# A transformer block on one core: tile 3's LayerNorm taken behind the start of K, scale sums ahead of tile 2's transposes, a matmul pair split 3 to 5

## Chip, cores, metric

One core of one Trainium2 chip. The time is the device time of a whole execution in microseconds.

Engines: PE (TensorE) multiplies, DVE (VectorE) and ACT (ScalarE) work on elements, POOL (GpSimd) does a few small operations, SP issues the loads.

## The reference, cut to what matters

A diffusion-transformer block on 2 batches of 256 tokens, width D = 1152, two heads, hidden width 4 D:

```python
mod = (_silu(c) @ w_mod).reshape(B, 6, 1, D)
shift_a, scale_a, gate_a, shift_m, scale_m, gate_m = [mod[:, i] for i in range(6)]
h = _layernorm(x) * (1 + scale_a) + shift_a
qkv = (h @ wqkv).reshape(B, N, 3, H, Dh)
# ... attention, output projection, second LayerNorm, two-layer MLP
```

Only the first 20 us matter here: LayerNorm of four 128-token tiles (0 and 1 are batch 0, 2 and 3 batch 1), their transposes, the scale sums `silu(c) @ w_mod` for `scale_a`, and the first matmuls of K, the key projection. A k-tile is one of the nine slices of 128 features over which these matmuls sum.

## The kernel before: the parts concerned

The builder keeps one list of instructions per engine and puts semaphore waits between them. PE runs exactly in the order in which the program names its units; the early orders of DVE and ACT are fixed by lists. Waits are per PSUM bank (PSUM is where PE's results land). `hk` multiplies one k-tile by its scale, and K's matmuls read its result. The program of PE before (cuts marked `...`):

```python
def sca(k0, k1):            # scale sums of weight rows k0..k1: 4 tiny matmuls per row
    for kt in range(k0, k1): mod_f0(kt)                  # feature tile 0, bank 1
    for kt in range(k0, k1): mod_kt(WSC, kt, 0, ..., (1, KC))  # tiles 1 to 3, bank 7
...
xn_T(1); sca(0, 3); warm(1, "d"); sca(3, 6); warm(1, "f", "aggr_ln1_2")
xn_T(0)                     # nine 128x128 transposes of normalised tile 0 into PSUM
warm(1, "e", "rstd_ln1_2")  # a filler matmul that keeps the clock up
xn_T(2, 0, 8)
sca(6, 9)
hk(0, 0); sc1a(0, 1, 1); sc1a(1, KC); hk(1, 0)   # DVE: scale batch 0; copy the sums
xn_T_copy(0, 4, 8, "act"); xn_T_copy(0, 8, 9, "act")       # ACT: read banks 5 and 3
hk(2, 0, "act"); hk(3, 0, "act")
xn_T(3, 0, 8)
k_first(0)                  # K, k-tile 0, batch 0: 8 matmuls into banks 0, 1, 5, 3
xn_T(3, 8, 9); xn_T(2, 8, 9)
k_first(1)
...
k_pair(range(KC), 0, 1); k_pair(range(KC), 1, 1); ...; k17(0, 0, KC)
for kt in range(KT):        # sums of the other scale features ("scb"): 9 x 5 tiny matmuls
    if kt == 6: k12(0)      # 4 matmuls of K, batch 1
    mod_kt(WSC, kt, 0, "scb_%d" % kt, (KC, KT))
hk(KC, 0)                   # DVE: scale k-tile 4, needs all the sums
...
k12(1)                      # the other 4
... k_pair((KC,), ...)      # K on k-tile 4
```

SP issues the loads in this order: x (two loads), the first half of the scale weights (`sc0`, three), K's weights for k-tiles 0 to 3, the second half of the scale weights (`sc4`, three), K's others, and so on.

Of the kernel before, what the change touches and what calls it, by code (L numbers as in the profile page):

```python
# [509 lines left out]
KC = 4  # L510
# [3 lines left out]
def c_mm(n):  # L514
    return max(n / 2.4 + 2.5, 27.0)
# [26 lines left out]
def build_kernel(nc, x, c, wqkv, wo, w_mod, w_fc1, w_fc2, out):  # L542
    S = Sched()
# [4 lines left out]
    with (  # L548
# [10 lines left out]
        def ps32(bank, c0=0, n=512):  # L559
            return psum[:, bank * 512 + c0: bank * 512 + c0 + n]  # L560
# [126 lines left out]
        def mm(o, l, r, st, sp, **kw):  # L687
            S.instr(lambda e: e.matmul(o, lhsT=l, rhs=r, start=st, stop=sp, **kw), reads=[l, r], writes=[o])  # L688

        def tr(o, i_, idn):  # L690
            S.instr(lambda e: e.transpose(o, i_, idn), reads=[i_, idn], writes=[o])  # L691
# [75 lines left out]
        def xslot(b, kt, n=256):  # L767
            return ps16(XB[b][kt // 4], (kt % 4) * 256 + (512 if kt == 8 and b == 1 else 0), n)


        def xn_T(t, ka=0, kb=KT):
            b = t // 2
            S.unit("pe", (kb - ka) * c_mm(128), "xnT_%d_%d" % (t, ka))
            for kt in range(ka, kb):
                tr(xslot(b, kt)[:, (t % 2) * 128:(t % 2) * 128 + 128], XN[:, t, kt * 128:(kt + 1) * 128], IDENT)

        def xn_T_copy(b, k0, k1, eng):
            src = xslot(b, k0, (k1 - k0) * 256).rearrange("p (k t) -> p k t", k=k1 - k0)
            copy_on(eng, HX[:, k0:k1, b * 256:(b + 1) * 256], src, (k1 - k0) * 256, True, "xnT_cp%d_%d" % (b, k0))

        def warm(n, tag, behind=None):
            for i in range(n):
                S.unit("pe", 300.0, "warm_%s_%d" % (tag, i))
                mm(ps32(0), IDENT, Q4B, True, True)
                if behind:
                    S.instrs[-1].deps.update(j for j in S.instrs[:-1] if j.name == behind)

        def mod_kt(W, kt, col0, name, fs=(0, 9)):
            S.unit("pe", (fs[1] - fs[0]) * 27.0, name)
            for f in range(*fs):  # L790
                mm(ps32(7, col0 + f * 2, 2), W[:, kt, f * 128:(f + 1) * 128], ST[:, kt:18:9], False, kt == KT - 1, skip_group_check=True)
# [6 lines left out]
        def hk(kt, b, eng="dve"):  # L798
            dst = HK[:, kt, b * 256:(b + 1) * 256]
            s1 = ps32(1 if kt == 0 else 7, 2 * kt, 1) if kt in (0, KC) and b == 0 else SC1A[:, kt * 2 + b:kt * 2 + b + 1]  # L800
            src = xslot(b, kt) if kt < KC else HX[:, kt, b * 256:(b + 1) * 256]
            if eng == "act":
                act(c_act(256, 1), lambda e: e.activation(out=dst, in_=src, func=ACTF.Copy, scale=s1), [src, s1], [dst], "hk_%d_%d" % (kt, b))
                return
            dve(345 if kt < KC else 285, lambda e: e.tensor_scalar(out=dst, in0=src, scalar1=s1, scalar2=None, op0=ALU.mult),  # L805
                [src, s1], [dst], "hk_%d_%d" % (kt, b))

        def k_mm(kts, j, b, bank, half):

            for kt in kts:  # L810
                mm(ps32(bank, half * 256, 256), WK[:, kt, j * 128:(j + 1) * 128], HK[:, kt, b * 256:(b + 1) * 256], kt == 0 and half == 0,
                   kt == KT - 1, skip_group_check=True)

        KB = [(0, 1, 5, 3), (4, 2, 6)]
        ev_rr = [0]

        def k_pair(kts, i, b, bank=None):
            S.unit("pe", 2 * len(kts) * c_mm(256), "k%d_%d_%d" % (b, i, kts[0]))
            bank = KB[b][i] if bank is None else bank
            if kts[0] == 0:  # L820
                for kt in kts:
                    for half in range(2):
                        k_mm((kt,), 2 * i + half, b, bank, half)
            else:
                for half in range(2):
                    k_mm(kts, 2 * i + half, b, bank, half)
            if kts[-1] == KT - 1:
                eng = "act" if ev_rr[0] % 2 == 0 or (i, b) == (3, 1) else "dve"
                ev_rr[0] += 1
                copy_on(eng, QK[:, 9 + 2 * i:11 + 2 * i, b * 256:(b + 1) * 256], ps32(bank).rearrange("p (j t) -> p j t", j=2), 512, False,  # L830
                        "k_ev%d_%d" % (b, i))

        def mod_f0(kt):
            S.unit("pe", 27.0, "sca0_%d" % kt)
            mm(ps32(1, 0, 2), WSC[:, kt, 0:P], ST[:, kt:18:9], False, kt == KT - 1, skip_group_check=True)

        def sca(k0, k1):
            for kt in range(k0, k1):
                mod_f0(kt)
            for kt in range(k0, k1):  # L840
                mod_kt(WSC, kt, 0, "sca_%d" % kt, (1, KC))
# [14 lines left out]
        sca(3, 6)  # L856
        warm(1, "f", "aggr_ln1_2")
        xn_T(0)
        warm(1, "e", "rstd_ln1_2")
        xn_T(2, 0, 8)  # L860
        sca(6, 9)
        hk(0, 0)
        sc1a(0, 1, 1)
        sc1a(1, KC)
# [2 lines left out]
        xn_T_copy(0, 8, 9, "act")  # L867
        hk(2, 0, "act")
        hk(3, 0, "act")
        xn_T(3, 0, 8)  # L870

        def k_first(kt):
            for i in range(4):
                k_pair((kt,), i, 0)

        k_first(0)
        xn_T(3, 8, 9)
        xn_T(2, 8, 9)
        k_first(1)
        xn_T_copy(1, 4, 8, "act")  # L880
        xn_T_copy(1, 8, 9, "act")
        for kt in range(2, KC):
# [6 lines left out]
        def k17(b, ka, kb):  # L889
            S.unit("pe", (kb - ka) * c_mm(256), "k17_%d_%d" % (b, ka))  # L890
            for kt in range(ka, kb):
                mm(ps32(7, 256 * (1 - b), 256), WK[:, kt, D - P:D], HK[:, kt, b * 256:(b + 1) * 256], b == 1 and kt == 0, kt == KT - 1,
                   skip_group_check=True)

        sc_ones(KC, KT)
        k17(0, 0, KC)
        def k12(half):
            S.unit("pe", KC * c_mm(256), "k1_2%d" % half)
            k_mm(range(KC), 4 + half, 1, KB[1][2], half)

        for kt in range(KT):
            if kt == 6:
                k12(0)
            mod_kt(WSC, kt, 0, "scb_%d" % kt, (KC, KT))
        hk(KC, 0)
        sc1a(KC, KT)
        for kt in range(KC, KT):
            for b in range(2):
                if kt > KC or b:
                    hk(kt, b)  # L910
        k12(1)
        for kt in range(KT):
            dma(WQ[:, kt, :], wqkv_v[:, kt, 0:D], P * D * 2, "ld_wq%d" % kt, run=2304)
# [44 lines left out]
        for kt in range(KT):  # L958
            for b in range(2):
# [5 lines left out]
                else:  # L965
# [4 lines left out]

        S.first = {
            "dve": ["zq4b", "c_half", "c_silu", "bn_ln1_1_0", "bn_ln1_1_1", "bn_ln1_1_2", "aggr_ln1_1", "veps_ln1_1", "bn_ln1_2_0",
                    "bn_ln1_2_1", "xn_1", "bn_ln1_2_2", "aggr_ln1_2", "veps_ln1_2", "xn_0", "var_ln1_3", "xn_2", "xn_3", "hk_0_0", "sc1a_0", "sc1a_1", "hk_1_0",
                    "hk_0_1", "hk_1_1", "hk_2_1", "hk_3_1", "hk_%d_0" % KC, "sc1a_4", "hk_%d_1" % KC] + ["hk_%d_%d" % (kt, b) for kt in range(KC + 1, KT) for b in range(2)],
            "act": ["ld_c", "c_tanh", "sum_ln1_0", "sq_ln1_0", "sum_ln1_3", "sq_ln1_3", "xnT_cp0_4", "xnT_cp0_8", "hk_2_0", "hk_3_0",
                    "xnT_cp1_4", "xnT_cp1_8"],
# [344 lines left out]
def bass_standalone__dit_block__diffusion_kernel(  # L1321
    nc: bass.Bass,
    x: bass.AP,
    c: bass.AP,
    wqkv: bass.AP,
    wo: bass.AP,
    w_mod: bass.AP,
    w_fc1: bass.AP,
    w_fc2: bass.AP,
    out: bass.AP,  # L1330
):
    build_kernel(nc, x, c, wqkv, wo, w_mod, w_fc1, w_fc2, out)
# [28 lines left out]
```

## Time and profile before

| | before |
|---|---|
| first three runs | 244.45 us median (244.39 to 244.59) |
| span of the profile | 242.9 us |
| k_first(0) starts | 12.116 us |
| first matmul on k-tile 4 | 20.226 us |
| from there to the end of the last DVE operation | 221.16 us |

Times inside a profile count from the start of the span. The two matmul starts are read from the trace's single records. A "hole" below is the time that PE stands still beyond the usual step from one matmul to the next; a load's "landing" is the moment at which its semaphore tells that its data are there. The prediction below shows the profile lines that led to it. Starts of transposes, weight loads and waits there are on the same clock.

### The profile page before, as it was taken

Reading aid. Unit: us, or ns where it says so; the run is one execution under the profiler, and the core shown is the slowest. Engines: PE = TensorE matmul, PEld = TensorE weight load, DVE = VectorE, ACT = ScalarE, POOL = GpSimd, SP = SyncE. Lnnn points to the kernel's source line nnn. Section 1 sums busy time; section 2 is a strip of 40 time slices with the busy share of each in tenths; the row PEclk is TensorE's granted clock in tenths of the full one; section 3 lists DMA queues with packets and bytes.
Section 4 is the critical chain, followed back from the end, with each engine's and each line's share of the span. In section 5 each row is a group of like instructions: output and inputs, shape, how many; then the busy total and the mean of one; then the engine's idle time right before and its main releaser. Section 6 shows DMA issues by size and latency. Waiting matters only on the chain.

```text
span 242.9 us, 4068 instructions
## 1 busy us (share of the span) xinstructions
PE 238.3 (98%) x1754; PEld 147.9 (61%) x1764; DVE 120.4 (50%) x218; ACT 67.0 (28%) x136; POOL 21.7 (9%) x39
## 2 busy tenths in 40 slices
PE   7999999999999999999999999999999999999996
PEld 2698854557667666898444444444556656566576
DVE  3824379596997899779999600000022222211112
ACT  4830350345424206983223332222000000000000
POOL 1600000000021186400000000020000000000000
DMA  6999999999995999989943498002000000000001
GB/s 236 338 381 392 391 391 391 398 413 404 390 353 165 345 388 392 391 262 398 338 148 84 170 302 330 0 15 86 0 16 19 16 16 19 16 16 16 19 21 30
DMA packets 30140, 51.59 MB, mean 212 GB/s; under 512 B 1703, under 2 KB 15787, under 8 KB 30123
## 3 DMA queue, kind: packets, MB, share of 16 engines
q1 hardware_dynamic: 29680, 50.14, 57.8%
q0 software_dynamic: 416, 1.19, 1.6%
q8 instruction: 14, 0.23, 0.4%
q14 instruction: 3, 0.02, 0.0%
q10 hardware_dynamic: 27, 0.00, 0.0%
HBM read 50.14 MB, written 1.19 MB: 211 GB/s over the span
## 4 chain that ended last, share of the span: by engine, by line
PE 94%; ACT 2%; DMA 2%; DVE 1%; issue 0%; POOL 0%; DVEq 0%
PE psum L688 93%; DMA arena<-in_x_dram 2%; PE psum L691 1%; ACT arena L749 1%; ACT arena L747 1%; POOL arena L751 0%; DVE arena L760 0%; DVE arena L805 0%; DVE arena L1284 0%; DVE arena L1285 0%; DVE arena L750 0%; DVEq L473 0%
## 5 line engine op out<-in xcount | busy, mean ns | idle before, releaser
L688 PE MATMUL psum<-arena 128*128 128x384 bf16 (+12 forms) x1665 | 234.8, 306 | 2.0 <-POOL arena L711 1.5
L688 PEld LDWEIGHTS psum<-arena 128*128 128x128 bf16 (+3 forms) x1675 | 142.7, 97 | 89.7 <-issue 4.5
L1079 DVE SCALAR_TENSOR_TENSOR arena<-arena 128x1152 f32<-128x1152 bf16 x32 | 44.7, 1414 | 0.6
L1284 DVE TENSOR_TENSOR arena<-psum,arena 128x384 f32<-128x384 f32 (+3 forms) x14 | 7.0, 501 | 68.0 <-PE psum L688 68.0
L1193 ACT ACTIVATE arena<-psum 128x512 bf16<-128x512 f32 (+1 forms) x44 | 22.4, 520 | 42.7 <-PE psum L688 42.7
L683 ACT ACTIVATE arena<-psum 128x512 bf16<-128x512 f32 (+6 forms) x37 | 19.6, 550 | 39.1 <-PE psum L688 38.2
L685 DVE CAST arena<-psum 128x512 bf16<-128x512 f32 (+3 forms) x13 | 8.2, 641 | 11.4 <-PE psum L688 11.3
L669 POOL DMA_DIRECT2D dit_scratch<-arena x3 | 1.8, 616 | 115.7 <-DVE arena L685 58.9
L1161 POOL TENSOR_TENSOR arena<-arena 128x384 f32<-128x384 f32 x12 | 10.9, 912 | 11.5 <-DVE arena L1160 9.8
L1106 DVE CAST arena<-psum 72x32 bf16<-72x32 f32 x1 | 0.2, 187 | 21.3 <-PE psum L688 21.3
L739 DVE BATCH_NORM_STATS2 arena<-arena 128x6 f32<-128x384 f32 (+1 forms) x18 | 9.4, 548 | 0.3
L1166 ACT ACTIVATE arena<-arena 128x1152 bf16<-128x1152 f32 x4 | 5.3, 1344 | 11.1 <-DVE arena L1165 11.1
L691 PEld LDWEIGHTS psum<-arena 128*128 128x128 bf16 (+1 forms) x89 | 5.8, 98 | 2.9 <-DVE arena L760 1.1
L691 PE MATMUL psum<-arena 128*128 128x128 bf16 (+1 forms) x89 | 7.3, 219 | 0.3
L1160 DVE TENSOR_TENSOR arena<-psum,arena 128x384 f32<-128x384 f32 x12 | 6.5, 552 | 1.5 <-PE psum L688 1.0
L1285 DVE TENSOR_TENSOR arena<-arena 128x384 bf16<-128x384 f32 (+3 forms) x14 | 7.0, 501 | 0.5
L1183 ACT ACTIVATE arena<-psum,arena 128x128 bf16<-128x128 bf16 x16 | 6.0, 456 | 1.7 <-PE psum L691 1.1
L1180 DVE TENSOR_SCALAR arena<-psum,arena 128x128 bf16<-128x128 bf16 x20 | 5.4, 337 | 1.9 <-PE psum L691 1.9
L1086 DVE TENSOR_REDUCE arena<-arena 128x36 f32<-128x1152 f32 x4 | 5.4, 1347 | 0.0
L1083 DVE STREAM_TRANSPOSE arena<-arena 128x1152 f32<-128x1152 f32 x4 | 5.4, 1364 | 0.0
L1009 ACT ACTIVATE arena<-psum,arena 128x256 bf16<-128x256 f32 x8 | 3.7, 472 | 1.3 <-PE psum L688 0.9
L743 POOL TENSOR_TENSOR arena<-arena 128x1 f32<-128x1 f32 x6 | 3.6, 596 | 1.6 <-DVE arena L742 1.6
(48 smaller groups left out, 45.0 us busy)
## 6 DMA issues: line engine op xcount, KB each, us to landing
arena<-in_w_fc_dram SPq DMA_DIRECT2D x9, 1152.0 KB, 7.2
arena<-in_w_fc_dram SPq DMA_DIRECT2D x4, 2592.0 KB, 17.4
arena<-in_wqkv_dram SPq DMA_DIRECT2D x18, 288.0 KB, 10.3
arena<-in_w_mod_dram SPq DMA_DIRECT2D x3, 1728.0 KB, 20.3
arena<-in_w_mod_dram SPq DMA_DIRECT2D x3, 864.0 KB, 13.9
arena<-in_w_mod_dram SPq DMA_DIRECT2D x9, 288.0 KB, 10.6
arena<-in_wqkv_dram SPq DMA_DIRECT2D x1, 2592.0 KB, 16.7
arena<-in_wo_dram SPq DMA_DIRECT2D x1, 2592.0 KB, 24.4
```

Source lines behind the costliest of these rows:

```text
L683: act(c_act(n), lambda e: e.activation(out=dst, in_=src, func=ACTF.Copy), [src], [dst], name)
L685: dve(c_dve_psum16(n) if psum16 else c_dve_psum32(n), lambda e: e.tensor_copy(dst, src), [src], [dst], name)
L688: S.instr(lambda e: e.matmul(o, lhsT=l, rhs=r, start=st, stop=sp, **kw), reads=[l, r], writes=[o])
L691: S.instr(lambda e: e.transpose(o, i_, idn), reads=[i_, idn], writes=[o])
L739: dve(550, lambda e, s=s, o=o: e.bn_stats(out=o, in_=s), [s], [o], "bn_%s_%d" % (tag, ci))
L1079: dve(1270, lambda e, w=w, s=s, acc=acc: e.scalar_tensor_tensor(out=acc, in0=w, scalar=s, in1=acc, op0=ALU.mult, op1=ALU.add), [w, s, acc] ...
L1160: dve(550, lambda e, o=o, ga=ga, x1c=x1c: e.tensor_tensor(out=x1c, in0=o, in1=ga, op=ALU.mult), [o, ga], [x1c], "wo_t1_%d_%d" % (t, ci))
L1161: S.op("pool", 930, lambda e, xs=xs, x1c=x1c: e.tensor_tensor(out=x1c, in0=x1c, in1=xs, op=ALU.add), reads=[x1c, xs], writes=[x1c], name=" ...
L1183: act(440, lambda e, o=o, dst=dst, s1=s1, s2=s2: e.activation(out=dst, in_=o, func=ACTF.Identity, scale=s1, bias=s2), [o, s1, s2], [dst], ...
L1193: act(c_act(ntok), lambda e: e.activation(out=dst, in_=o, func=ACTF.Gelu_apprx_tanh), [o], [dst], "gelu_%d_%d" % (f, tok0))
L1284: dve(c_dve_psum32(w), lambda e, o=o, gm=gm, t1=t1: e.tensor_tensor(out=t1, in0=o, in1=gm, op=ALU.mult), [o, gm], [t1], "fc2_t1_%d_%d" % ( ...
L1285: dve(c_dve_32(w), lambda e, t1=t1, x1c=x1c, ost=ost: e.tensor_tensor(out=ost, in0=t1, in1=x1c, op=ALU.add), [t1, x1c], [ost], "fc2_out_%d ...
```

## The change

Its intent is to let K start before tile 3 is normalised. The sums of rows 6 to 8 go ahead of tile 2's transposes, and the filler goes. Tile 3's normalise stands behind the scaling of batch 0 on DVE, and its transposes behind `k_first(1)`. One of four matmuls moves from before the last scale sums to behind them, where PE waits for DVE.

```diff
         xn_T(0)
-        warm(1, "e", "rstd_ln1_2")
+        sca(6, 9)
         xn_T(2, 0, 8)
-        sca(6, 9)
         hk(0, 0)
 ...
-        xn_T(3, 0, 8)
 ...
         k_first(0)
-        xn_T(3, 8, 9)
+        k_first(1)
         xn_T(2, 8, 9)
-        k_first(1)
+        xn_T(3)
 ...
-        def k12(half):
-            S.unit("pe", KC * c_mm(256), "k1_2%d" % half)
-            k_mm(range(KC), 4 + half, 1, KB[1][2], half)
+        def k12(part):
+            kts = ((range(3), ()), (range(3, KC), range(KC)))[part]
+            S.unit("pe", sum(map(len, kts)) * c_mm(256), "k1_2_part%d" % part)
+            for half in range(2):
+                k_mm(kts[half], 4 + half, 1, KB[1][2], half)
 ...
     DVE list:  - "xn_2", "xn_3", "hk_0_0", "sc1a_0", "sc1a_1", "hk_1_0",
                + "xn_2", "hk_0_0", "sc1a_0", "sc1a_1", "hk_1_0", "xn_3",
```

## The prediction

> **What bounds the kernel now.** I read the page first, then the chain of waits in order of time, then the timeline of each engine from 8 to 21 us, then the landings of the first loads.
>
> The chain that ended last is TensorE (PE) for 94% of the 242.9 us span. In order of time it looks like this around the part that the diff touches:
>
> ```profile
> 10.11 0.88 POOL arena L751
> ...
> 11.02 0.59 DVE arena L760
> 11.61 0.05 issue
> 11.66 0.62 PE psum L691 x8
> 12.28 0.87 PE psum L688 x8
> 13.15 0.11 PE psum L691 x2
> 13.26 6.62 PE psum L688 x95
> 19.89 0.29 DVE arena L805
> 20.18 0.05 issue
> 20.23 13.26 PE psum L688 x144
> ```
>
> Up to 11.61 us the end is set by tile 3's LayerNorm: POOL's rstd, DVE's normalise (L760), then its eight transposes (L691). From 11.66 us PE runs without a hole until 19.89, where one DVE scaling (hk of k-tile 4, L805) shows. After 20.23 the chain has no DMA in it, and nothing but a few 0.05 us pieces comes between the matmuls until the last output. So whatever the change saves before 20.23 should arrive at the end nearly whole, and the question is how much that is.
>
> PE's timeline before the dense part:
>
> ```profile
> 9.79 0.66 PE L691 MATMUL psum<-arena 128*128 128x128 bf16 x9
> 10.29 0.38 PE L688 MATMUL psum<-arena 128*128 128x512 bf16 x1
> 10.64 0.62 PE L691 MATMUL psum<-arena 128*128 128x128 bf16 x8
> 11.10 0.46 PE L688 MATMUL psum<-arena 128*128 128x2 bf16 x12
> 11.66 0.62 PE L691 MATMUL psum<-arena 128*128 128x128 bf16 x8
> ```
>
> That is: tile 0's transposes, one filler matmul ("warm e"), tile 2's eight transposes, the twelve scale sums sca(6,9), tile 3's eight transposes; then k_first(0) from 12.12. The weight loads show the idle time that the pipelined matmuls hide: the filler is followed by a wait, the scale sums by another, and there is a third at 20.22:
>
> ```profile
> 10.63 0.45 PEld L691 LDWEIGHTS psum<-arena 128*128 128x128 bf16 x8 [0.31 <-DVE arena L760]
> 11.65 0.45 PEld L691 LDWEIGHTS psum<-arena 128*128 128x128 bf16 x8 [0.20 <-DVE arena L760]
> 20.22 0.11 PEld L688 LDWEIGHTS psum<-arena 128*128 128x128 bf16 x2 [0.34 <-DVE arena L805]
> ```
>
> Start-to-start steps from the trace's single records: 56 ns a transpose, 109 ns a 128x256 matmul, 27 ns a 128x2 one, 216 ns the filler. Lost time by them: 10.285 + 0.216 to 10.639 is 0.138 us; the last sum at 11.389 + 0.027 to 11.659 is 0.243; 19.887 + 0.109 to 20.226 is 0.230.
>
> **What the Trainium skill says.** (1) "TensorE: Matmul & The Clock Gate", "Wait — 56ns, not 53.3ns?": N / 2.4 GHz + about 2.5 ns once warm, with a floor near 25 ns. The trace agrees (56, 109, 216 and 27 ns), so moving these instructions changes no cost; only holes count. (2) Same page, "What's actually happening": a clock at half rate until activity releases it, back after an idle window of about 3.4 us. The trace's 128x512 step falls from 427 to 216 ns at 6.4 us and never rises; dropping one filler leaves a hole of under 0.1 us, so I expect no slow clock. (3) Same page, "The cost: per-tile semaphore tail": increments serialise, 26.3 ns each. The trace's semaphore events agree in kind, 34 ns apart: the last scb matmul starts at 19.536, its increment comes at 19.853, and DVE's hk of k-tile 4 starts at 19.877. I use these offsets below. (4) "PSUM — Partial Sum Buffer", "PSUM bank collisions raise a hardware error": two engines must not be on one bank, so users guard by bank. The kernel does: K's four pairs write banks 0, 1, 5 and 3, and 5 and 3 hold the transposes that ACT is still copying. No wait of this kind shows before, but the new order meets one.
>
> **The change, part by part.** No arithmetic is added; one filler is removed.
>
> *Scale sums ahead of tile 2.* Tile 0's transposes end their turn at 10.285. The twelve sums then run 12 x 27 ns, to 10.605, where the filler and a wait stood. Their weights landed at 10.07, so this is free. Tile 2's transposes still wait for its normalise (semaphore at 10.592) and start at 10.64 as before, until 11.096. Saved here: the sums' own 0.32 us after tile 2.
>
> *Tile 3 leaves the path.* DVE finishes issuing tile 2's normalise at about 10.50. Next is now hk(0,0): the third sum increments at 10.285 + 0.211 + 2 x 0.034 = 10.564, hk runs 10.59 to 10.94 (0.349 as now). So k_first(0) can start when PE is free, at 11.096 instead of 12.116; its weights landed at 10.81. The copies sc1a follow at 10.86 and 10.92, hk(1,0) at 11.11 to 11.46, tile 3's normalise at 11.39 to 11.97.
>
> *The new wait.* ACT's two copies out of the transposes are unchanged:
>
> ```profile
> 10.48 1.30 ACT L683 ACTIVATE arena<-psum 128x1024 bf16<-128x1024 bf16 x2 [0.71 <-PE psum L691]
> ```
>
> The first ends at 11.508 (bank 5), the second at 11.783 (bank 3). PE comes to the pair in bank 5 at 11.096 + 4 x 0.109 = 11.532 and has to wait to about 11.56; to bank 3 at about 11.79 and waits to 11.835. With the slower first step after a wait, about 0.09 us is lost, and k_first(0) ends near 12.063 instead of 11.97.
>
> *Order after it.* k_first(1) needs hk(1,0) (11.46) and weights (11.57): no wait, ends 12.063 + 8 x 0.109 = 12.935. Ten transposes (tile 2's last, tile 3's nine; normalised by 11.97) take 0.56, so k_first(2) starts at 13.495 against 13.974: 0.479 us earlier. hk(2,0) and hk(3,0) on ACT are done by 12.7. Tile 3's copies and the hk of batch 1 end by about 15, ahead of their use from 15.2. So all up to the scb sums is rigidly 0.479 earlier: scb starts at 17.450.
>
> *K pair split 3 to 5.* Only three instead of four of its 109 ns matmuls stand ahead of the last fifteen scb sums, which therefore move from 19.163 to 18.578 (0.479 + 0.109 = 0.585 earlier with rounding). hk of k-tile 4 follows by the measured 0.714, at 19.29, and the first matmul on it by 0.349, at 19.64. Five matmuls after the sums fill PE to about 19.52, so the 0.230 hole becomes about 0.12.
>
> Sum: tile 3's waiting and the filler, 0.138 + 0.216 + 0.243 = 0.597; minus 0.09 to 0.12 for ACT's banks and small shifts; plus 0.109 from the smaller hole: 0.585 us. 244.45 - 0.585 = 243.87 us, a ratio of 0.9976.
>
> **The rivals.** *A DMA takes over.* The last fifteen sums read the load issued here:
>
> ```profile
> 7.42 0.94 SPq L669 DMA_DIRECT2D arena<-in_w_mod_dram  x1
> ...
> arena<-in_w_mod_dram SPq DMA_DIRECT2D x1, 480.0 KB, 11.1
> ```
>
> It lands at 18.51, 0.65 before its use now, and only 0.07 before the use I predict: a cap. PE gets the news some 0.04 later, so it could gain 0.61 at most, and each 0.1 us that the load is late is lost. That landing is already late: its two like-sized predecessors land 1.36 us apart, this one 2.73 after, with one 16 KB instruction packet of 1.15 us at 15.59 between. The fetch should move with PE and delay the same load. If the load came 0.3 later, 244.15. *ACT's banks cost more.* If bank 3 is freed 0.2 later, the loss comes straight off: 244.05. For it: ACT starts on tile 0's transposes and takes 1.30 us; against it: nothing in the diff delays it. *The shift is swallowed later.* The stream runs at about 390 GB/s whatever PE does. The last shift weights land at 29.00 against a use at 30.15, the first WQ slice at 29.76 against 33.53, its last at 41.83 against 43.9, WV at 49.36 against 53.2, the mod rows at 62.23 against 66.2. The smallest margin is 1.15 us, about twice the shift, so I expect nothing. If it happened: 244.4. *The static order changes elsewhere.* DVE's and ACT's later order comes from a model of time in the builder, which may swap a few instructions; the path is PE with holes of at most 0.05, so a swap would mostly be hidden. Up to 0.5 us either way. *Scale sums late.* If the increments queue more than assumed, hk(0,0) delays k_first(0); there is 0.10 us of room (10.99 against 11.096).
>
> **Range and chances.** Best case is the cap plus noise: 243.6. Bad but plausible is that half is lost and the noise of the runs before (244.39 to 244.59) goes against it: 244.3. The whole stretch is under 1% of the time, so a move of over 2% would need a mistake of another kind, such as a load or clock upset.
>
> **What would show it.** In the changed profile: tile 2's transposes still at 10.64; hk(0,0) near 10.59; k_first(0) near 11.10 directly behind them; two small PE waits on ACT near 11.55 and 11.83; ten transposes near 12.94; the last scb sums near 18.58; hk of k-tile 4 near 19.29 and PE going on near 19.64, with a hole near 0.12 rather than 0.23; a later identical shape, 0.58 us earlier. Wrong would be: a wait on a DMA near 18.5, a wait on ACT of over 0.2, hk(0,0) after 10.75, or new holes after 20 us.

## The result

| | before | changed | ratio |
|---|---|---|---|
| first result: runs | 244.38 us (243.73 to 244.59), 6 | 244.05 us (243.61 to 244.60), 6 | 0.9989 [0.9971, 1.0008] |
| again | 244.47 us, 11 | 244.24 us, 5 | 0.9993 [0.9981, 1.0005] |
| a third time | 244.24 us, 11 | 244.11 us, 5 | 0.9996 [0.9984, 1.0008] |
| span of the first profile | 242.9 us | 242.3 us | |

A ratio is the mean time of one kernel's fast runs over that of the other's in the same rounds, so not quite the ratio of the medians beside it; the brackets are its 95% interval. Of these times and the six of a rerun of before, the mean of the 16 of the changed kernel is 244.15 us and that of the 34 of before is 244.34: a gain of 0.19 us, give or take 0.19 by the two scatters (0.33 and about 0.25 us). (Nine more runs of before, from rounds without the changed kernel, have a mean of 244.56 and are left out.) So the kernel is about 0.2 us faster if it is faster at all: each of the three intervals includes 1, and all are within 2%. The median lies in the predicted range; the forecast of 0.585 us was about three times what the times show.

The first profile seems to say otherwise. The chain of waits of the changed kernel, in order of time (start, length, what):

```profile
10.32 0.47 PE psum L688 x12
10.80 0.47 PE psum L691 x8
11.26 1.83 PE psum L688 x16
13.09 0.56 PE psum L691 x10
13.65 45.25 PE psum L688 x382
```

LayerNorm of tile 3 is gone from it: the sums, tile 2's transposes, sixteen K matmuls, ten transposes, K, and no DVE scaling at 19.9 any more. DVE's timeline shows the new order, scaling first (L805), tile 3's normalise (L760) last:

```profile
10.61 0.35 DVE L805 TENSOR_SCALAR arena<-psum 128x256 bf16<-128x256 bf16 x1 [0.25 <-PE psum L688]
10.88 0.22 DVE L795 COPY arena<-psum 128x2 f32<-128x2 f32 x2
11.14 0.35 DVE L805 TENSOR_SCALAR arena<-psum,arena 128x256 bf16<-128x256 bf16 x1
11.41 0.57 DVE L760 TENSOR_SCALAR arena<-arena 128x1152 bf16<-128x1152 bf16 x1
```

The weight loads of PE show where it still waits (in brackets the idle time before and who ended it):

```profile
10.32 0.38 PEld L688 LDWEIGHTS psum<-arena 128*128 128x128 bf16 x12 [0.17 <-DMA arena<-in_w_mod_dram]
...
11.15 0.46 PEld L688 LDWEIGHTS psum<-arena 128*128 128x128 bf16 x5
...
19.62 0.22 PEld L688 LDWEIGHTS psum<-arena 128*128 128x128 bf16 x3 [0.24 <-DVE arena L805]
```

The sums at 10.32 now wait for a DMA, which they did not in the first profile of before, and the bracket before k-tile 4 is down from 0.34 to 0.24. From the single records: k_first(0) at 11.184 (predicted 11.10), ten transposes from 12.927 (12.94), last fifteen sums at 18.564 (18.58), k-tile 4 at 19.630 (19.64), the hole before it 0.123 (0.12). From 19.630 to the last element operation it is 221.162 us, against 221.164 before. Nearly every predicted time is met, and the profiled gain is 0.6 us. Yet two inputs had moved between the two profiles: x landed at 4.77 us before and 4.33 after, and K's first weights at 10.81 and 11.05. The latter by two views, the SP timeline and the DMA issues of that moment (KB, us to landing), first of before:

```profile
3.71 0.49 SPq L669 DMA_DIRECT2D arena<-in_wqkv_dram  x1
...
arena<-in_wqkv_dram SPq DMA_DIRECT2D x1, 288.0 KB, 7.1
```

then of the changed kernel:

```profile
3.37 0.53 SPq L669 DMA_DIRECT2D arena<-in_wqkv_dram  x1
...
arena<-in_wqkv_dram SPq DMA_DIRECT2D x1, 288.0 KB, 7.7
```

3.71 + 7.1 = 10.8 and 3.37 + 7.7 = 11.1: issued earlier, landed later. A difference of two single profiles therefore contains what the loads did in those two executions, and the experiments had to separate this from the change.

### The profile page after: what moved, and what is told of

Its sections match the earlier page's. It is cut to its first block, busy times and chain, and to the rows that moved or that the text cites. A ratio compares the mean times of both kernels' runs of the same rounds, so it can differ in the third digit from the quotient of the medians.

```text
span 242.3 us, 4076 instructions
## 1 busy us (share of the span) xinstructions
PE 238.4 (98%) x1763; PEld 147.5 (61%) x1763; DVE 120.3 (50%) x218; ACT 67.0 (28%) x136; POOL 21.2 (9%) x39
## 4 chain that ended last, share of the span: by engine, by line
PE 97%; DVE 2%; POOL 0%; issue 0%; ACT 0%; DVEq 0%; POOLq 0%
PE psum L688 95%; PE psum L691 2%; DVE arena L739 1%; DVE arena L760 0%; POOL arena L711 0%; DVE arena L740 0%; DVE arena L1284 0%; DVE arena L1285 0%; POOL arena L710 0%; ACT arena L726 0%; DVE arena L727 0%; DVE arena L732 0%; DVE arena L742 0%; POOL arena L717 0%; POOL arena L715 0%
## 5 line engine op out<-in xcount | busy, mean ns | idle before, releaser
L688 PE MATMUL psum<-arena 128*128 128x384 bf16 (+10 forms) x1674 | 234.9, 306 | 1.6 <-POOL arena L711 1.5
L1161 POOL TENSOR_TENSOR arena<-arena 128x384 f32<-128x384 f32 x12 | 10.9, 910 | 10.8 <-DVE arena L1160 9.5
```

What stands on the lines that cost most here:

```text
L688: S.instr(lambda e: e.matmul(o, lhsT=l, rhs=r, start=st, stop=sp, **kw), reads=[l, r], writes=[o])
L1161: S.op("pool", 930, lambda e, xs=xs, x1c=x1c: e.tensor_tensor(out=x1c, in0=x1c, in1=xs, op=ALU.add), reads=[x1c, xs], writes=[x1c], name=" ...
```

## The experiments

My theory: before, K's start is set by tile 3's normalise, hence by x; after the change it is set by the landing of K's first weights, so the gain is the distance of two things that scatter from run to run. Rivals: each part brings its own share whatever lands when; or the gain is lost later.

All twelve gave correct results. Times from the single records of each trace, in us; "weights" is the landing of K's weights for k-tile 0, "norm 3" the end of tile 3's normalise:

| kernel | x | weights | norm 3 | k_first(0) | k-tile 4 | to the last DVE operation |
|---|---|---|---|---|---|---|
| before, first profile | 4.77 | 10.81 | 11.60 | 12.116 | 20.226 | 221.164 |
| before_again | 4.25 | 11.18 | 11.01 | 11.636 | 19.742 | 221.162 |
| only_sums | 5.08 | 11.83 | 11.90 | 12.415 | 20.522 | 221.167 |
| only_split | 4.87 | 11.35 | 11.70 | 12.210 | 20.213 | 221.162 |
| only_tile3 | 4.79 | 11.43 | 13.01 | 12.054 | 20.622 | 221.164 |
| before_late_ln3 | 4.75 | 11.25 | 12.08 | 12.596 | 20.707 | 221.163 |
| before_wkswap | 4.77 | 12.63 | 11.60 | 12.763 | 20.868 | 221.164 |
| changed, first profile | 4.33 | 11.05 | 11.98 | 11.184 | 19.630 | 221.162 |
| after_again | 4.73 | 11.10 | 12.06 | 11.230 | 19.764 | 221.163 |
| after_third | 4.84 | 11.33 | 12.39 | 11.485 | 20.085 | 221.166 |
| after_late_ln3 | 4.80 | 11.35 | 12.39 | 11.632 | 20.084 | 221.165 |
| after_split44 | 4.65 | 11.20 | 12.16 | 11.340 | 19.951 | 221.165 |
| after_split26 | 4.38 | 11.63 | 12.55 | 11.767 | 20.179 | 221.164 |
| after_wkswap | 4.76 | 12.09 | 12.29 | 12.229 | 20.676 | 221.165 |

The last column is the plainest finding: from the first matmul on k-tile 4 to the last DVE operation it takes the same time to 5 ns in all fourteen traces, whatever happened ahead of it. The rival "lost later" is out.

### Both kernels again

No edit. The first profiles were one sample each.

> The changed kernel, unaltered, to see whether the 0.6 us of its trace is there in repeated times. Theory (the shift is carried to the end, run-to-run scatter comes from when the loads land): ratio to before 0.9970 to 0.9985, and in the trace the first matmul on k-tile 4 between 19.5 and 19.8 us with the span 0.5 to 0.7 us under that of before. Rival (the second half of the scored runs was right, the gain is lost in most executions): ratio 0.9993 to 1.0005 and a trace in which that matmul is no earlier than 20.0 us or a hole appears after it.

Measured: ratio 0.9993 [0.9981, 1.0005]; k-tile 4 at 19.764. The span, 243.0, was no shorter than before's 242.9, though k-tile 4 and the last DVE operation came 0.46 us earlier. The difference is in the tail behind that operation, the wait for the last output stores: 2.08 us here, 1.52 in before's first profile, 1.49 to 2.08 over the fourteen. So the tail is one more source of scatter, and the expectation of a span 0.5 to 0.7 shorter failed by it. The ratio is inside the expectation and close to the rival's, whose other half, k-tile 4 no earlier than 20.0, did not come.

> The kernel before against itself: the scatter of the method. Expected ratio 0.999 to 1.001; trace with the first matmul on k-tile 4 at 20.15 to 20.35 us. If x lands at another time than 4.77 us, theory (before is set by LayerNorm, so by x) says that matmul moves by the same amount; the rival (before is set by the weights' stream already) says it does not.

Measured: ratio 0.9996 [0.9984, 1.0007]. x landed 0.52 us earlier than in the first profile, and k-tile 4 came at 19.742, 0.484 earlier, although K's weights landed 0.37 later. So the old kernel follows x, but not by the wait that the theory names: k_first(0) is 0.626 behind tile 3's normalise instead of 0.515, and PE's weight loads wait for tile 2 (10.41) but not for tile 3 (11.17):

```profile
10.41 0.45 PEld L691 LDWEIGHTS psum<-arena 128*128 128x128 bf16 x8 [0.31 <-DVE arena L760]
10.82 0.42 PEld L688 LDWEIGHTS psum<-arena 128*128 128x128 bf16 x12
11.17 0.46 PEld L691 LDWEIGHTS psum<-arena 128*128 128x128 bf16 x8
```

Tile 2's transposes start 0.22 us earlier than in the first profile, and the hole of 0.243 before tile 3's, a term of the prediction's sum, is gone. That term is one draw. This unlucky sample for the change would have made it look worthless, as the first pair made it look worth 0.6.

> The changed kernel once more, beside the three others. Theory: k_first(0) 0.136 us behind the landing of its weights whatever x does, 8.45 us (8.56 if the last scale weights are late) to the first matmul on k-tile 4, 221.16 us from there to the end; ratio to before 0.9983 to 0.9998, which with the two sets of times so far would put the mean gain at 0.1 to 0.4 us. Rival (the 0.585 us of the prediction is what it brings on average): ratio 0.9970 to 0.9980.

Measured: ratio 0.9996 [0.9984, 1.0008], in the band and far from the rival's. k_first(0) is 0.152 behind its weights, and 8.60 us pass to k-tile 4, more than the 8.56 that I allowed. In that trace PE itself came late: the second load of x landed at 7.01 (5.74 to 6.51 in the other thirteen), the first transposes stood at 8.65, and tile 2's ended only when the weights' news came. And the two waits on ACT's PSUM copies that the prediction named are there, in the weight loads:

```profile
12.00 0.11 PEld L688 LDWEIGHTS psum<-arena 128*128 128x128 bf16 x2 [0.20 <-ACT arena L683]
12.27 0.22 PEld L688 LDWEIGHTS psum<-arena 128*128 128x128 bf16 x3 [0.16 <-ACT arena L683]
```

They cost 0.082 and 0.046 us beyond the usual step. So guarding the banks is paid with 0.13 us in this trace, with 0.05 in after_again, and in the first profile not at all.

### Is it the weights? Two loads swapped

```diff
-            for kt in range(ka, kb):
+            for kt in ((1, 0, 2, 3) if ka == 0 else range(ka, kb)):
                 dma(WK[:, kt, :], ...)
```

> The changed kernel with the loads of K's weights for k-tiles 0 and 1 in swapped order, so that tile 0 lands one load (0.75 us) later. Theory now (with the change the start of K is held by the landing of its first weights, 0.136 us from landing to matmul in three traces): k_first(0) starts 0.136 us after that landing, near 11.9 to 12.1, and the first matmul on k-tile 4 comes 0.6 to 0.8 later than in the changed kernel, near 20.3 to 20.6; ratio to before 1.0005 to 1.0030. Rival (the normalise and scaling chain on DVE, or ACT's copies, still set it): no later than the changed kernel, ratio below 0.9998.

Measured: ratio 1.0008 [0.9995, 1.0021], k-tile 4 at 20.676. PE's timeline:

```profile
10.97 0.61 PE L691 MATMUL psum<-arena 128*128 128x128 bf16 x8
12.23 0.38 PE L688 MATMUL psum<-arena 128*128 128x256 bf16 x2 [0.65 <-DMA arena<-in_wqkv_dram]
```

After tile 2's transposes PE stands still until the load has landed: 12.093 in the trace, and k_first(0) at 12.229, 0.136 later. That same distance is found in the first profile (11.048 to 11.184), after_again (0.135), after_split44 and after_split26 (0.136): five traces, landings over a range of 1.0 us. So in the changed kernel the weights can hold K's start; this part of the theory is shown. How long they hold it is another matter: the hole before k_first(0) is 0.81 us here, but 0.083 in the first profile, 0.068 in after_again and nothing in after_third.

> The kernel before with the same swap. Theory (before is held by x through tile 3's LayerNorm, its first weights have up to 1 us of room): k_first(0) within 0.2 us of where tile 3's normalise puts it (0.515 us behind its end), ratio 0.9993 to 1.0010. Rival (before is held by the weights too): later by about 0.7 us, ratio 1.002 to 1.004.

Measured: ratio 1.0004 [0.9991, 1.0018], in the band; but the trace's half of the expectation failed. k_first(0) came at 12.763, 0.135 behind its weights and 0.64 behind where the normalise would have put it (11.604 + 0.515 = 12.12). The load stream was late in that execution (the last of the first scale weights at 11.12; median of the traces 10.59). My "up to 1 us of room" came from the first profile, 12.116 - 10.81 - 0.136 = 1.17. With the median landing of all fourteen, below, it is about 0.64 (12.116 - 11.34 - 0.136), and one load of 0.75 eats it. PE came late as well: the second of the first scale loads held it for 0.75 us until 10.0, and of the 0.64 us only the hole of 0.289 before k_first(0) is the wait for K's weights.

### Is it LayerNorm no longer? Half a microsecond more of it

```diff
+            if tag == "ln1_3":
+                act(500, ... activation(out=junk[:, 0:CH], in_=src[:, 0:CH], func=Identity) ...)
             act(1250, ... Square ... accum_out=msq ...)
```

> The kernel before with one more ACT instruction of about 0.5 us in tile 3's LayerNorm. Theory (tile 3's normalise holds the start of K in it): k_first(0) stays 0.515 us behind the end of that normalise, both about 0.5 us later than without it, first matmul on k-tile 4 at 20.6 to 20.8 for x at 4.75; ratio to before 1.0008 to 1.0028. Rival (the weights' stream holds it): k_first(0) 0.136 us behind its weights' landing, ratio under 1.0006.

Measured: ratio 1.0014 [1.0002, 1.0026], normalise until 12.080, k_first(0) at 12.596 (0.516 behind), k-tile 4 at 20.707. ACT's timeline shows what was put in, 0.52 us:

```profile
8.50 0.52 ACT L751 ACTIVATE arena<-arena 128x384 bf16<-128x384 bf16 x1
```

and nearly the whole of it arrives at PE: 20.707 against 20.226 at the same landing of x (4.75 and 4.77), 0.481. That LayerNorm's lateness reaches PE is shown; that it is tile 3's alone is not, since the extra instruction delayed tile 2's normalise too (until 11.06 instead of 10.58; the reason follows under after_late_ln3). That tile 3's is the last to hold PE is read from its transposes, which wait once more after tile 2's (a hole of 0.240):

```profile
12.13 0.23 PEld L691 LDWEIGHTS psum<-arena 128*128 128x128 bf16 x4 [0.19 <-DVE arena L763]
```

> The changed kernel with the same extra ACT instruction. Theory (tile 3 has left the path, with about 0.9 us of room before its transposes): no change from the changed kernel, k_first(0) 0.136 us behind the landing of its weights, 8.45 us from it to the first matmul on k-tile 4 (up to 8.56 if the last scale weights land late), no PE wait at the ten transposes; ratio to before 0.9983 to 1.0000. Rival (the normalise still counts): 0.3 us or more later, ratio 1.0005 or more.

Measured: ratio 1.0002 [0.9990, 1.0014], a little over the band and 0.0006 above the changed kernel's in the same rounds; k_first(0) 0.282 behind its weights instead of 0.136. The theory held on its main point, since tile 3's transposes wait for nothing and 8.452 us pass to k-tile 4. But "no change" was wrong by 0.146 us, and DVE's timeline says why:

```profile
10.47 0.16 DVE L753 TENSOR_TENSOR arena<-arena 128x1 f32<-128x1 f32 x1 [0.87 <-ACT arena L752]
10.54 0.57 DVE L763 TENSOR_SCALAR arena<-arena 128x1152 bf16<-128x1152 bf16 x1
```

Tile 3's small variance operation (L753) stands ahead of tile 2's normalise (L763) in DVE's list. When ACT is late with tile 3, DVE waits 0.87 us and delays tile 2, which does hold PE. So tile 3's LayerNorm left PE's path, but one instruction of it still sits in front of something on it.

### The parts alone

> One part alone: scale sums 6 to 8 ahead of tile 2 and the filler gone, all else as before. Theory: nothing gained (ratio 0.9995 to 1.0005; first matmul on k-tile 4 within 0.05 us of before's in its own trace, relative to tile 3's normalise), because tile 3's normalise still holds PE until 11.66 and the 0.32 us of sums only turn into a longer hole there. Rival (each part brings its own share): about 0.25 us earlier.

The edit is the diff's first hunk. Measured: ratio 0.9992 [0.9980, 1.0004], a little under the band I gave, though not distinguishable from before. The trace decides: there k_first(0) is 0.515 behind tile 3's normalise, exactly before's distance. Moving the sums gains nothing while the normalise holds PE (in before_again's execution it did not). Its weight loads show a cost as well, because in this execution the scale weights came at 11.08:

```profile
11.12 0.38 PEld L688 LDWEIGHTS psum<-arena 128*128 128x128 bf16 x12 [0.52 <-DMA arena<-in_w_mod_dram]
11.43 0.98 PEld L691 LDWEIGHTS psum<-arena 128*128 128x128 bf16 x16
```

The sums in front of tile 2 make its transposes wait for a DMA. Here tile 3 hid it.

> One part alone: tile 3 behind hk of batch 0 and behind K's second k-tile, but the filler kept, the scale sums behind tile 2 and the split 4 to 4. Theory: a loss. The sums end at about 11.42, hk(0,0) starts near 11.40 and ends near 11.75, so k_first(0) starts near 11.80, and the ten transposes come after k_first(1): k_first(2) near 14.1 against 13.97, first matmul on k-tile 4 0.10 to 0.18 later than before at the same landing of x (20.3 to 20.4 for x at 4.75); ratio 1.0000 to 1.0012. Rival (this part carries most of the gain): 0.3 us or more earlier, ratio below 0.9990.

The edit is the diff's second hunk and the DVE list; filler and sums stay. Measured: ratio 1.0001 [0.9989, 1.0014]: no gain, in the band, where the rival had below 0.9990. k_first(0) came at 12.054 instead of 11.80 and k-tile 4 at 20.622, 0.4 later than in before's first profile instead of 0.10 to 0.18. The weight loads:

```profile
11.28 0.42 PEld L688 LDWEIGHTS psum<-arena 128*128 128x128 bf16 x12
12.05 1.64 PEld L688 LDWEIGHTS psum<-arena 128*128 128x128 bf16 x16 [0.35 <-DVE arena L805]
13.70 0.65 PEld L691 LDWEIGHTS psum<-arena 128*128 128x128 bf16 x10
```

With the sums behind tile 2, K waits for DVE's scaling of batch 0 instead of tile 3, and the ten transposes come on top. The 0.25 us beyond my number is another matter: the fillers ran at half speed until 7.74 us here (steps of 427 ns, then 216), which held the first transposes to 8.60 against 8.20 in before's first profile. In the fourteen traces the first full fast step begins anywhere from 4.69 to 8.01 us. The Trainium skill, "TensorE: Matmul & The Clock Gate" ("What's actually happening"), says that the window that releases the clock is free-running, 3413 ns long, and that the transition varies by 500 ns either way; here it varies by 3.3 us, nearly one whole window.

So neither of these two parts gained alone in its trace: only both together let K start when its weights are there.

> One part alone: K pair split 3 to 5. Theory: 0.109 us earlier than before at the same landing of x: first matmul on k-tile 4 at 20.10 to 20.13 for x at 4.77, hole before it 0.12; 8.00 us from k_first(0) to it against 8.11 of before; ratio 0.9988 to 1.0003. Rival (capped by the landing of the last first-half scale weights): the 8.11 stays.

(The "last first-half scale weights" here and under after_split26 can only be the last load of the second half, the one that the prediction calls a cap.) The edit is the diff's third hunk. Measured: ratio 0.9991 [0.9979, 1.0004]; 8.003 us from k_first(0) to k-tile 4 against 8.110 of before, the hole 0.12 instead of 0.23. (k-tile 4 itself, at 20.213, is later than the stated 20.13 because x landed 0.09 later.) The time alone shows nothing at this size; the trace shows the 0.107 us, because that distance hardly moves (8.105 to 8.111 in the five other traces with tile 3 in its old place).

> The changed kernel with the K pair split 4 to 4 again. Theory: the last fifteen scale sums 0.109 us later than in the changed kernel, first matmul on k-tile 4 at 19.70 to 19.78 us, hole before it 0.23 instead of 0.12; ratio to before 0.9975 to 0.9990. Rival (the weights' landing near 18.5 caps it, so the split brings nothing): no difference from the changed kernel at that matmul.

The third hunk undone. Measured: ratio 0.9989 [0.9977, 1.0001], the hole 0.229 as expected. k-tile 4 came at 19.951, outside the 19.70 to 19.78 that I had fixed without allowing for the loads: its weights were 0.16 later than in the first profile. From k_first(0) it took 8.611 us against 8.446 in the first profile: 0.109 of that is the split, the rest 0.045 on an ACT bank wait and about 0.01 on smaller steps.

### A version that might beat it: 2 to 6

```diff
-            kts = ((range(3), ()), (range(3, KC), range(KC)))[part]
+            kts = ((range(2), ()), (range(2, KC), range(KC)))[part]
```

> The changed kernel with the K pair split 2 to 6. Theory: where the last first-half scale weights land early, the last fifteen sums come 7.27 us behind k_first(0) instead of 7.38, the hole before k-tile 4 falls from 0.12 to about 0.02, and the first matmul on k-tile 4 comes 8.34 us behind k_first(0); where they land late it comes 1.11 us behind that landing, as in the changed kernel, and nothing is gained. Ratio to before 0.9980 to 0.9998, at most 0.0005 under the changed kernel's.

Measured: ratio 0.9992 [0.9979, 1.0006], in the band. The sums came 7.273 behind k_first(0), as expected, but the hole only fell to 0.09 and k-tile 4 came 8.412 behind, not 8.34:

```profile
20.18 0.11 PEld L688 LDWEIGHTS psum<-arena 128*128 128x128 bf16 x2 [0.20 <-DVE arena L805]
```

DVE's scaling began 0.792 us behind the first of the fifteen sums instead of 0.69 to 0.72 in the other thirteen traces. PE's semaphore events in the traces say why. Each matmul increments one semaphore; the sums start every 27 ns but increment it every 34 ns, and DVE starts 0.024 us behind the last sum's increment. With four matmuls before the last sums there are 49 increments from the first sum's to the last one's, with one pause (a step of 0.107 us in before): there the matmuls set the pace. With three there are 48 without a pause (in the first profile of the changed kernel), and with two 47, again without: there the increments set it, and a matmul less saves one step of 34 ns. That is "The cost: per-tile semaphore tail" of the Trainium skill's page "TensorE: Matmul & The Clock Gate" at work, with 34 ns here against its 26.3. The gain left over is 0.03 us, which no timing here can resolve. The split of 3 is nearly as good as any.

## Why the prediction was right or wrong

- **Right: the mechanism and the places.** Tile 3's normalise held PE in the profile that was read, and with the same 0.51 to 0.52 us to k_first(0) in only_sums, only_split and before_late_ln3, though not in before_again, nor in before_wkswap, where its transposes did not wait either; sums, scaling of batch 0, k_first, ten transposes followed in the predicted order. The extra LayerNorm shows that its lateness arrived at PE (0.481 of 0.52 us), the table shows that no shift is lost later (221.16 us in all traces, before a tail of stores that no kernel here changes). A path of PE without holes was a safe reason to say so.
- **Right: the split.** 0.109 predicted, 0.107 measured in only_split.
- **Partly right: ACT's banks.** About 0.09 us predicted; 0.00, 0.05 and 0.13 in the three traces of the changed kernel.
- **The step whose size failed: "k_first(0) can start when PE is free, at 11.096 instead of 12.116; its weights landed at 10.81", and with it the sums' "Their weights landed at 10.07, so this is free".** Both landings were taken from one profile, and both were the earliest of fourteen: K's weights land between 10.81 and 11.87, median 11.34; the scale weights between 10.07 and 11.12, median 10.59. (In the swapped kernels the first position of K's loads is counted here.) Landing plus 0.136 is 11.48 at the median, so the start is 0.4 us later than forecast. An estimate from these numbers: changed, 11.48 + 8.45 to 8.60 is 19.93 to 20.08; before, with the normalise ending at 11.60 as at x's landing of 4.77, 11.60 + 0.515 + 8.11 is 20.23: a gain of 0.15 to 0.30. The times give 0.19 ± 0.19. The rival "a DMA takes over" was the right one to name, but I tied it to the second-half scale weights alone. They held PE visibly only in after_again (0.04 us). Measured, k_first(0) came at 11.184, 11.230 and 11.485 in the three traces, 0.09 to 0.39 us later than forecast: partly by K's weights (holes of 0.083, 0.068 and 0.00), in the first profile also by the scale weights (0.164 at 10.32), in the third because PE's chain came late. On the other side of the sum, the 0.243 us of waiting for tile 3 that the change was to save was 0.00 in before_again. How the shortfall divides among these on average is not shown.
- **Right by accident: 19.64.** The first profile hit it because weights 0.09 us too late and ACT's missing wait of 0.09 cancelled. Agreement of a total in one trace was no proof of its terms.
- **The range held** for the noise allowance rather than for its reasoning: the times of one kernel spread over about 1 us, more than the change.

What stays open: why x lands anywhere from 4.25 to 5.08 us and the weights anywhere in 1.1 us, with the first packets at 1.79 to 1.82 in every trace. And the mean gain itself is known only to about 0.2 us.

## What to carry to other kernels

Before taking a wait off the path, ask what is the next thing that the path will meet, and how much that thing moves between executions: a landing read from one profile is one draw, and the margin to it shrinks by the whole of what you gain. Where a change is smaller than the scatter of times, compare distances inside the trace (landing to first use, one matmul to another) rather than medians or two spans; here they were steady to 5 ns while times spread over about 1 us. Parts that each remove one of two parallel holds can show nothing alone, so judge them together.

## What the Trainium skill lacked or had wrong

- "TensorE: Matmul & The Clock Gate", "What's actually happening": the transition to the fast clock is given as varying by 500 ns either way, though the section also warns that the count of slow matmuls varies by run; in these fourteen traces it fell between 4.69 and 8.01 us.
- Same page, "The cost: per-tile semaphore tail": 26.3 ns per increment for packed tiles; increments of ordinary 128x2 matmuls came 34 ns apart, behind starts 27 ns apart, so a run of thirty builds up a delay of about 0.2 us for whoever waits.
- "DMA: Bandwidth & Descriptors", "Latency and other measured facts", gives an average HBM latency and one for high load, but not how much a landing in a busy stream varies from execution to execution: the sixth load of a fixed sequence landed between 10.81 and 11.87 us in fourteen traces.
- No page that I read gives the time from a load's landing to a matmul that waits for it: 0.135 to 0.136 us for K's first matmul in five traces of the changed kernel and its variants, 0.045 to 0.047 for the scale sums in the first profile, after_split26 and after_wkswap. In the traces a semaphore instruction and a second wait stand in front of the former, one wait in front of the latter.
